# Soft-MoE after squared-ReLU attention: logits turned to slot rows in fp32, raw z for the first chunk, and the last half key tile in three products

## The chip, the cores and the metric

The kernel runs on one NeuronCore of a Trainium2 chip. The time is that of one execution on the device in microseconds; the median of three runs before the change is 1592.67 us. Engines are named as in the profile: PE (TensorE matrix products; PEld is its weight loads), DVE (VectorE), ACT (ScalarE), POOL (GpSimd) and SP (the queue that issues the DMAs). On PE one operand, the weights, is loaded into the 128 x 128 array and the other, the moving operand, streams through it. The array is used here mostly as two halves of 64 rows, which run separate products side by side, and in places as eight tiles of 64 x 32.

## The reference

```python
# B, S, D, d_qk = 8, 2496, 256, 64 ; E = 8 experts of 4 slots, F = 1024
scores = z @ z.T / S                    # per batch, (S, S)
attn = maximum(scores, 0) ** 2
x = u * (attn @ v)                      # (B*S, D) tokens, N = 19968
logits = x @ phi                        # (N, 32)
d = exp(logits - logits.max(0));  d /= d.sum(0) + 1e-9      # over tokens, per slot
slot_input = d.T @ x                    # (32, D)
slot_out[e] = maximum(slot_input[e] @ w1[e], 0) @ w2[e]     # 4 slots per expert
c = exp(logits - logits.max(1));  c /= c.sum(1) + 1e-9      # over slots, per token
out = c @ slot_out
```

All arrays are fp32. Everything up to `slot_input` is done in one pass over the tokens with running column maxima.

## The kernel before

**Split products.** Where speed matters, an fp32 operand is split into a rounded part of type fp32r (high) and the rest (low), and a product is three fp32r products: high x high, high x low, low x high. `load_z` (L70) and `load_v` (L83) load a raw tile and return a function that splits it: the high part is an ACT copy, the low part a DVE subtraction. z comes from the host as 64 rows twice (`zz`), so each half of the array has a copy; v comes in key tiles of 128, of which the 20th (`KT - 1`) holds the last 64 keys twice.

**Chunks and steps.** A batch's 2496 queries are worked in chunks of 512 and one of 448 (in the last batch 448 first, and the last 512 as two of 256). For a chunk there are five steps of four key tiles. `scores` (L184) computes two key tiles against the chunk, one in each half of the array, three products each, then ACT's Relu and Square and DVE's split into `ph` and `pl`. `attend` (L217) adds the products of v with `ph` and `pl` into the accumulator `acc`. It goes through a step's key tiles twice, in two turns `s`: a half of the array holds 64 of the 128 keys, and in the second turn the halves exchange the output columns, which lie in two banks of PSUM, PE's output memory. A turn's first product waits, through an empty POOL instruction, for the last product of the turn before (L233, L245 to L248). A key tile is three products for a half in each turn. For the 20th key tile the rows 64 to 127 of `ph` are overwritten with the low part (L213), and the half of rows 0 to 63 has two products in each turn and the other half one (L229, L230).

**Order.** `pe`, `act` and `dve` keep the order in which the program issues (`InOrder`, L38). Before each turn `between` (L478) runs the deferred DVE operations in `begin`, takes at most one item from `work`, and then issues a pair of scores of the *next* step with `pair` (L434). `middle` is run on ACT between the Relus and the Squares of the pair, `behind` after them. From the third turn of a chunk on one item of `work` is taken a turn, so up to eight a chunk.

**Opening.** `opening` and `next_split` (L95 to L104) load and split the first batch's z and v tiles between the first steps, with three raw tiles ahead. The second operand of the first chunk's scores is the split z tile 0, the weights are the split tile of the step.

**Tokens in groups.** `finish_chunk` (L274) multiplies the accumulator by u (with x's features on the partitions) and splits x into `xh` and `xl`. Tokens are taken in groups of 512, g = 0 to 38. A group has eight work items. Four are `group_tile` (L306): eight fp32r products with a matrix `rmat`, which holds an identity and phi, and turn a tile of 128 tokens and give its 32 logits at once; ACT copies both out (`lg`, `xt`), DVE adds up the logits (`lt`). One is empty. Three are steps of `group_soft` (L342): the maxima over a group's tokens by a transpose (`cmT`), spread back by another (`mbT`), exponentials `ex` and the combine weights `cw`, then the slot sums `sl`: eight fp32 products in 64 x 32 tiles of the array, added into `slot_acc` under the factor `al` for the change of the running maximum. All of this uses one PSUM buffer, `ms`.

**End.** `slot_acc` is summed over its four token tiles by products with the selection `esel` into `sT` (L514), the experts' two layers follow (`layer1`, `layer2`), `turn` (L402) transposes the combine weights, and `tokens` multiplies and stores 20 MB of output.

## Time and profile before

| | |
|---|---|
| median of three runs | 1592.67 us (1591.65 to 1595.54) |
| profiled execution | 1589.23 us, its span 1587.4 us |
| PE busy | 1534.9 us, 97% |
| DVE busy | 1258.0 us, 79% |
| ACT busy | 1103.6 us, 70% |
| slot products `sl` | 624 instructions, 26.0 us |
| products of the token tiles `tr` | 1248 instructions, 201.6 us |
| first attention product | starts at 15.92 us |
| end of the last product with u to the sums `sT` | 1499.04 to 1509.94 us |

A PE duration in the profile goes from the issue to the modelled end, so durations of products that run side by side or one behind the other overlap; what a product costs is read from the starts of its neighbours. An fp32 product is two instructions, an fp32r product and a transpose one. L46 is a helper's line through which all ordered instructions go, so operations are told apart by their tiles: `acc` attention, `sc` scores, `tr` token tiles, `sl` slot sums, `cT` the transposes of `turn`, `cmT` and `mbT` the maxima.

### The profile page before, as it was taken

How to read it: one execution, taken by the hardware profiler on the slowest of the kernel's cores; microseconds unless marked ns; L12 is line 12 of the kernel's file. 1: busy time of each engine (PE TensorE's matmuls, PEld its weight loads, DVE VectorE, ACT ScalarE, POOL GpSimd, SP SyncE). 2: the span in 40 equal slices, each digit the busy share in tenths (PEclk: the TensorE clock that was granted, in tenths of full speed). 3: DMA queues.
4: the chain of work that ended last, by engine and by line, in shares of the span. 5: the costliest groups of instructions: out<-in, count | busy, mean ns of one | idle time of the engine just before them, and what ended most of it. 6: DMA issues, size and time to landing. Idle time of an engine off the chain costs nothing.

```text
span 1587.4 us, 37236 instructions
## 1 busy us (share of the span) xinstructions
PE 1534.9 (97%) x14686; PEld 1300.1 (82%) x14686; DVE 1258.0 (79%) x2714; ACT 1103.6 (70%) x2346; POOL 3.3 (0%) x20
## 2 busy tenths in 40 slices
PE   6999999999999999999999999999999999999985
PEld 4787888889888888889888898888988889888853
DVE  6778877889779887888778887788878888777753
ACT  5677766778668776777667776677767777666543
POOL 0000000000000000000000000000000000000000
PEclk9999999999999999999999999999999999999985
DMA  3101110112001110111001120011100131000659
GB/s 120 48 21 46 55 34 15 35 46 68 21 15 46 48 48 14 28 46 55 28 15 41 47 67 15 20 47 48 42 14 28 46 119 43 26 8 8 232 217 388
DMA packets 36654, 91.55 MB, mean 58 GB/s; under 512 B 3712, under 2 KB 6272, under 8 KB 34432
## 3 DMA queue, kind: packets, MB, share of 16 engines
q1 hardware_dynamic: 36480, 89.18, 17.4%
q8 instruction: 116, 1.90, 0.5%
q14 instruction: 58, 0.48, 0.1%
HBM read 68.71 MB, written 20.45 MB: 56 GB/s over the span
## 4 chain that ended last, share of the span: by engine, by line
PE 86%; DVE 7%; DMA 2%; ACT 2%; issue 2%; DVEq 0%; SPq 0%; ACTq 0%
PE acc L46 62%; PE sc L46 16%; PE tr L46 5%; DMA outT<-ot 2%; DVE z L46 2%; DVE ph L46 1%; PE sl L46 1%; ACT r L46 1%; DVE pl L46 1%; PE h L542 1%; DVE x L46 0%; PE po L564 0%; DVE slot_acc L46 0%; DVE ot L624 0%; DVE v L46 0%
## 5 line engine op out<-in xcount | busy, mean ns | idle before, releaser
L46 PE MATMUL acc<-ph,v 64*128 64x512 f32 (+2 forms) x6464 | 1094.8, 382 | 0.7 <-DVE ph L46 0.7
L46 PEld LDWEIGHTS acc<-ph,v 64*128 64x128 f32 x6464 | 782.1, 184 | 90.3 <-DVE ph L46 1.8
L46 PE MATMUL acc<-pl,v 64*128 64x512 f32 (+2 forms) x3110 | 789.6, 381 | 0.0
L46 ACT ACTIVATE r<-sc 128x512 f32<-128x512 f32 (+2 forms) x820 | 428.4, 575 | 264.2 <-PE sc L46 253.1
L46 DVE TENSOR_TENSOR pl<-r,ph 128x512 fp32r<-128x512 f32 (+2 forms) x779 | 519.0, 666 | 51.8 <-PE acc L46 0.5
L46 DVE CAST ph<-r 128x512 fp32r<-128x512 f32 (+2 forms) x820 | 334.9, 408 | 205.4 <-ACT r L46 202.2
L46 PEld LDWEIGHTS acc<-pl,v 64*128 64x128 f32 x3110 | 448.0, 184 | 46.6 <-DVE pl L46 2.0
L46 ACT ACTIVATE r<-r 128x512 f32<-128x512 f32 (+2 forms) x820 | 455.2, 611 | 0.0
L46 PE MATMUL sc<-z,z 64*128 64x512 f32 (+2 forms) x1968 | 325.3, 389 | 12.4 <-ACT z L46 7.3
L46 PEld LDWEIGHTS sc<-z,z 64*128 64x128 f32 x1968 | 213.4, 185 | 44.8 <-issue 12.9
L46 ACT COPY lg<-tr 128x128 f32<-128x128 f32 x156 | 41.2, 264 | 124.6 <-PE tr L46 124.2
L46 PE MATMUL tr<-rmat,xl 64*128 64x256 f32 x624 | 100.0, 281 | 5.5 <-DVE xl L46 5.4
L46 PE MATMUL tr<-rmat,xh 64*128 64x256 f32 x624 | 101.6, 280 | 1.3 <-DVE slot_acc L46 1.3
L46 PEld LDWEIGHTS tr<-rmat,xh 64*128 64x128 f32 x624 | 84.9, 184 | 9.9 <-PE acc L46 3.3
L46 PE MATMUL sc<-z 64*128 64x512 f32 (+2 forms) x492 | 82.8, 395 | 5.3 <-ACT z L46 4.1
L46 PEld LDWEIGHTS tr<-rmat,xl 64*128 64x128 f32 x624 | 74.5, 184 | 10.8 <-DVE xl L46 8.5
L46 PEld LDWEIGHTS sc<-z 64*128 64x128 f32 x492 | 53.9, 188 | 13.6 <-ACT z L46 4.1
L46 DVE TENSOR_REDUCE lt<-lg 128x32 f32<-128x128 f32 x156 | 59.7, 383 | 0.8 <-ACT lg L46 0.5
L46 ACT COPY xt<-tr 128x256 f32<-128x256 f32 x156 | 59.0, 378 | 0.0
L46 DVE TENSOR_TENSOR v<-vr,v 128x512 fp32r<-128x512 f32 x80 | 54.8, 686 | 4.1 <-ACT v L46 3.8
L46 ACT CAST v<-vr 128x512 fp32r<-128x512 f32 x80 | 49.4, 617 | 12.0 <-PE sc L46 12.0
L46 DVE TENSOR_TENSOR z<-zr,z 64x512 fp32r<-64x512 f32 x80 | 55.0, 687 | 2.5
(81 smaller groups left out, 675.7 us busy)
## 6 DMA issues: line engine op xcount, KB each, us to landing
vr<-in_v SPq DMA_DIRECT2D x80, 256.0 KB, 2.6
w<-in_w SPq DMA_DIRECT2D x32, 512.0 KB, 5.6
outT<-ot SPq DMA_DIRECT2D x16, 1024.0 KB, 8.3
ut<-in_uT SPq DMA_DIRECT2D x31, 512.0 KB, 3.6
zr<-in_zz SPq DMA_DIRECT2D x40, 256.0 KB, 2.6
ut<-in_uT SPq DMA_DIRECT2D x8, 448.0 KB, 3.4
outT<-ot SPq DMA_DIRECT2D x4, 512.0 KB, 4.6
outT<-ot SPq DMA_DIRECT2D x2, 768.0 KB, 5.6
```

The lines of the kernel that those rows point to most:

```text
L46: return lambda *a, **k: self.tc.keep_in_program_order(f(*a, **k))
L542: nc.tensor.matmul(ps[j * NS : (j + 1) * NS], sT[:, c, (4 * eg + j) * NS : (4 * eg + j + 1) * NS], w_raw[w][:, k], start=(c == 0), stop=(c ...
```

## The change

- The last half key tile: the low part goes to a buffer of its own, and the three products of its 64 keys are dealt out so that both halves have two in the first turn and one in the second.
- The first chunk's scores are fp32 products of raw z tiles, all five of which stay in memory; their splits are issued later in the first and early in the second chunk, and only the v splits stand between the first steps.
- x is no longer split. Per group there are four work items in the place of eight. First the logits as 32 slots x 128 tokens, the four token tiles on four bands of 32 partitions (`lg`), with a maximum kept for each slot of each band; then the transposes of x (`tr`); then the transposes of logits and exponentials (`le`); then `sl` as before.
- The running maxima differ from band to band, so at the end a factor (`fac`) brings the four bands to one maximum, and `esel` times this factor (`fsel`) takes its place.
- x's columns come out in another order, and the host turns w1's rows accordingly.

```diff
-    zt, vt_ = {}, {}
+    zt, vt_, zraw = {}, {}, {}
     def load_z(b, j):
-        raw = raws.tile([P, 512], F32, tag="raw", name=f"zr_{b}_{j}")
+        raw = raws.tile([P, 512], F32, tag="zraw" if b == 0 else "raw", name=f"zr_{b}_{j}", bufs=NQ if b == 0 else NRAW)
         nc.sync.dma_start(raw, zz[b, :, j * 512 : (j + 1) * 512])
+        zraw[b, j] = raw
         def split():
             t = zt[b, j] = blk.tile([P, 2, 512], F32R, tag="blk", name=f"z_{b}_{j}")
             for h in (1, 0):
                 rows = HALF[h]
-                (dve.tensor_copy if h and b + j == 0 else act.copy)(t[rows, h], raw[rows])
+                act.copy(t[rows, h], raw[rows])
                 dve.tensor_sub(t[rows, 1 - h], raw[rows], f32(t[rows, h]))
         return split
...
-        raw = raws.tile([P, 2, D], F32, tag="raw", name=f"vr_{b}_{i}")
+        raw = raws.tile([P, 2, D], F32, tag="raw", name=f"vr_{b}_{i}", bufs=NRAW)
...
-    opening = [(load_z, 0)]
+    opening = []
     for p in range(NP):
-        opening += [(load_v, 2 * p), (load_v, 2 * p + 1)] + [(load_z, p + 1)] * (p + 1 < NP)
-    opened = []
-    def next_split():
-        while opening and len(opened) < NRAW - 1:
+        opening += [(load_z, p), (load_v, 2 * p), (load_v, 2 * p + 1)]
+    z_splits, v_splits = [], []
+    def open_loads(m):
+        while opening and (len(v_splits) < m or opening[0][0] is load_z):
             f, j = opening.pop(0)
-            opened.append(f(0, j))
-        opened.pop(0)()
+            (z_splits if f is load_z else v_splits).append(f(0, j))
...
-    rmat = xpool.tile([P, 2, 256], F32R, name="rmat")
-    NXT = 6
-    xt = [xpool.tile([P, 258], F32, name=f"xt{i}") for i in range(NXT)]
+    one = cpool.tile([1, 1], F32, name="one")
+    xt = [xpool.tile([P, 4, 258], F32, name=f"xt{i}") for i in range(2)]
...
         j, o, n, t0 = ch
         k0 = 4 * p + 2 * w
         ps = [sc_ps.tile([P, QC], F32, tag="sc", name=f"sc_{t0}_{k0 + h}") for h in range(2)]
-        zk, zq = zt[b, p], zt[b, j]
-        for m, (kl, ql) in enumerate(((0, 0), (0, 1), (1, 0))):
+        if t0 == 0:
             for h, rows in enumerate(HALF):
                 c = 2 * w + h
                 pe.matmul(
-                    ps[h][:, :n], zk[rows, h ^ kl, c * P : (c + 1) * P],
-                    zq[rows, h ^ ql, o : o + n], start=(m == 0), stop=(m == 2),
+                    ps[h], zraw[b, p][rows, c * P : (c + 1) * P], zraw[b, 0][rows],
+                    start=True, stop=True,
                 )
+        else:
+            zk, zq = zt[b, p], zt[b, j]
+            for m, (kl, ql) in enumerate(((0, 0), (0, 1), (1, 0))):
+                for h, rows in enumerate(HALF):
+                    c = 2 * w + h
+                    pe.matmul(
+                        ps[h][:, :n], zk[rows, h ^ kl, c * P : (c + 1) * P],
+                        zq[rows, h ^ ql, o : o + n], start=(m == 0), stop=(m == 2),
+                    )
         rs = []
         for h in range(2):
             r = wa.tile([P, QC], F32, tag="r", name=f"r_{t0}_{k0 + h}", bufs=5)
...
-            if kt < KT - 1:
+            if t0 == N - 256 and kt == KT - 1:
+                lo, rows = hi, HALF[1]
+            else:
                 lo = wa.tile([P, QC], F32R, tag="pl", name=f"pl_{t0}_{kt}", bufs=7)
-                dve.tensor_sub(lo[:, :n], r[:, :n], f32(hi[:, :n]))
-            else:
-                lo = None
-                dve.tensor_sub(hi[64:128, :n], r[64:128, :n], f32(hi[64:128, :n]))
+                rows = HALF[1] if kt == KT - 1 else slice(0, P)
+            dve.tensor_sub(lo[rows, :n], r[rows, :n], f32(hi[rows, :n]))
             pend[t0, kt] = hi, lo
         run(behind)
...
         j, o, n, t0 = ch
-        todo = [[], []]
+        todo = [[[], []], [[], []]]
         for kt in range(4 * p, 4 * p + 4):
             hi, lo = pend.pop((t0, kt))
             vt = vt_[b, kt // 2][:, kt % 2]
-            if lo is not None:
-                for h in range(2):
-                    todo[h] += [(vt[:, 0], hi), (vt[:, 1], hi), (vt[:, 0], lo)]
+            hh, lh, hl = (vt[:, 0], hi), (vt[:, 1], hi), (vt[:, 0], lo)
+            if kt < KT - 1:
+                for s in range(2):
+                    for h in range(2):
+                        todo[s][h] += [hh, lh, hl]
             else:
-                todo[0] += [(vt[:, 0], hi), (vt[:, 1], hi)]
-                todo[1] += [(vt[:, 0], hi)]
+                todo[0][0] += [hh, lh]
+                todo[0][1] += [lh, hl]
+                todo[1][0] += [hh]
+                todo[1][1] += [hl]
         for s in range(2):
             between(s)
             before = turns[-1:]
-            for i in range(len(todo[0])):
+            for i in range(len(todo[s][0])):
                 for h, rows in enumerate(HALF):
-                    if i >= len(todo[h]):
-                        continue
-                    vp, pp = todo[h][i]
+                    vp, pp = todo[s][h][i]
                     c = h ^ s
                     x = pe.matmul(
                         acc[:, c, :n], vp[rows, c * P : (c + 1) * P], pp[rows, :n],
                         start=(p == 0 and s == 0 and i == 0),
-                        stop=(p == NP - 1 and s == 1 and i == len(todo[h]) - 1),
+                        stop=(p == NP - 1 and s == 1 and i == len(todo[s][h]) - 1),
                     )
                     while before:
                         await_(x, before.pop())
...
-    xparts = {}
+    xg_ = {}
     def finish_chunk(b, ch, acc):
         _, _, n, t0 = ch
         ut = ut_.pop(t0)
-        x = wa.tile([P, 2, QC], F32, tag="x", name=f"x_{t0}", bufs=1)
-        dve.tensor_mul(x[:, :, :n], acc[:, :, :n], ut[:, :, :n])
         s = 0
         while s < n:
             g, o = divmod(t0 + s, 512)
             w = min(n - s, 512 - o)
-            if g not in xparts:
-                xparts[g] = tuple(
-                    wk.tile([P, 2, 512], F32R, tag=f"x{k}", name=f"x{k}_{g}") for k in "hl"
-                )
-            xh, xl = (t[:, :, o : o + w] for t in xparts[g])
-            xs = x[:, :, s : s + w]
-            def high(xh=xh, xl=xl, xs=xs):
-                act.copy(xh, xs)
-                begin.append(lambda: dve.tensor_sub(xl, xs, f32(xh)))
-            behind.append(high)
-            for t in range(o // P, (o + w) // P):
-                work.append(lambda g=g, t=t: group_tile(g, t))
+            if g not in xg_:
+                xg_[g] = wk.tile([P, 2, 512], F32, tag="xg", name=f"xg_{g}")
+            dve.tensor_mul(xg_[g][:, :, o : o + w], acc[:, :, s : s + w], ut[:, :, s : s + w])
             if o + w == 512:
-                it = group_soft(g)
-                work.extend([lambda: None] + [lambda it=it: next(it, None)] * 3)
+                it = group(g)
+                work.extend([lambda it=it: next(it, None)] * 4)
             s += w
...
+    def group(g):
+        x = xg_.pop(g)
+        ps = ms_ps.tile([P, 2, 512], F32, tag="ms", name=f"lg_{g}")
         for c in range(2):
...
+            for t in range(4):
                 for h, rows in enumerate(HALF):
                     pe.matmul(
...
+                        ps[t * NS : (t + 1) * NS, h, 0:P], phi_sb[rows, c],
+                        x[rows, c, t * P : (t + 1) * P], start=(c == 0), stop=(c == 1),
                     )
...
+        L = wk.tile([P, P], F32, tag="L", name=f"L_{g}")
+        E = wk.tile([P, P], F32, tag="E", name=f"E_{g}")
+        m = wk.tile([P, 4], F32, tag="m", name=f"m_{g}")
         mnew, mold = runmax[g % 2], runmax[(g + 1) % 2]
+        dve.tensor_copy(L, ps[:, 0, 0:P])
+        dve.tensor_add(L, L, ps[:, 1, 0:P])
         if g == 0:
...
+            dve.reduce_max(mnew, L, axis=AX.X)
         else:
...
+            dve.reduce_max(m[:, 0:1], L, axis=AX.X)
+            dve.tensor_max(mnew, m[:, 0:1], mold)
+            dve.tensor_sub(m[:, 2:3], mold, mnew)
+        dve.tensor_scalar_mul(m[:, 1:2], mnew, -1.0)
         def exps():
...
+            act.activation(E, L, AF.Exp, bias=m[:, 1:2])
             if g:
...
+                act.activation(m[:, 3:4], m[:, 2:3], AF.Exp)
         middle.append(exps)
         yield
...
+        ps = ms_ps.tile([P, 2, 512], F32, tag="ms", name=f"tr_{g}")
         for t in range(4):
+            for c in range(2):
+                for h, rows in enumerate(HALF):
+                    pe.transpose(
+                        ps[:, h, t * P + c * 64 : t * P + (c + 1) * 64],
+                        x[rows, c, t * P : (t + 1) * P], ident[rows, rows],
+                    )
+        xs = xt[g % 2]
+        act.copy(
+            xs[:, :, 0:D].rearrange("p t (h q) -> p h t q", h=2),
+            ps.rearrange("p h (t q) -> p h t q", q=P),
+        )
+        yield
+        ps = ms_ps.tile([P, 2, 512], F32, tag="ms", name=f"le_{g}")
+        for k, m_ in enumerate((L, E)):
+            for h, rows in enumerate(HALF):
+                pe.transpose(ps[:, h, k * 64 : (k + 1) * 64], m_[rows], ident[rows, rows])
+        le = wk.tile([P, 2, P], F32, tag="le", name=f"le_{g}")
+        act.copy(le, ps[:, :, 0:P])
+        rm = wk.tile([P, 2, 4], F32, tag="rm", name=f"rm_{g}")
+        lt = le[:, :, 0:64].rearrange("p h (b s) -> p h b s", s=NS)
+        cg = cw[:, g].rearrange("p (h b s) -> p h b s", b=2, s=NS)
+        def rows_of(i):
+            return rm[:, i].rearrange("p (h b) -> p h b", b=2)
+        def spread(i):
+            return rows_of(i).unsqueeze(3).to_broadcast([P, 2, 2, NS])
+        def combine():
+            dve.tensor_reduce(rows_of(0), lt, axis=AX.X, op=ALU.max)
+            dve.tensor_sub(cg, lt, spread(0))
+            middle.append(combine_exp)
+        def combine_exp():
+            act.activation(cw[:, g], cw[:, g], AF.Exp)
+            begin.append(combine_sum)
+        def combine_sum():
+            dve.tensor_reduce(rows_of(1), cg, axis=AX.X, op=ALU.add)
+            dve.tensor_scalar_add(rm[:, 1], rm[:, 1], 1e-9)
+            dve.reciprocal(rm[:, 1], rm[:, 1])
+            dve.tensor_mul(cg, cg, spread(1))
+        begin.append(combine)
+        yield
+        ps = ms_ps.tile([P, 2, 512], F32, tag="ms", name=f"sl_{g}")
+        for t in range(4):
+            e = le[:, t // 2, 64 + t % 2 * NS : 64 + (t % 2 + 1) * NS]
             for h, rows in enumerate(HALF):
                 pe.matmul(
...
+                    ps[t * NS : (t + 1) * NS, h, 0:258], e[rows], xs[rows, t], start=True, stop=True
                 )
         snew, sold = slot_acc[g % 2], slot_acc[(g + 1) % 2]
         if g == 0:
...
+            dve.tensor_copy(snew, ps[:, 0, 0:258])
         else:
             dve.scalar_tensor_tensor(
...
+                snew, sold, m[:, 3:4], ps[:, 0, 0:258], op0=ALU.mult, op1=ALU.add
             )
...
+        dve.tensor_add(snew, snew, ps[:, 1, 0:258])
...
-            next_split()
-            if w and opened:
-                next_split()
-    next_split()
+            v_splits.pop(0)()
+            open_loads(NRAW)
+        if b == 0 and z_splits and q % 2 and t0 + q >= 5:
+            z_splits.pop(0)()
+    open_loads(NRAW)
     for w in range(2):
         pair(0, w)
     constants()
...
     ep = ctx.enter_context(tc.tile_pool(name="ep", bufs=1))
     sfin = slot_acc[(NG - 1) % 2]
+    mfin = runmax[(NG - 1) % 2]
+    pm = ms_ps.tile([P, 512], F32, tag="ms", name="pm")
+    nc.tensor.transpose(pm[0:1, 0:P], mfin, ident)
+    mrow = ep.tile([1, 5, NS], F32, name="mrow")
+    nc.vector.tensor_reduce(
+        mrow[:, 4], pm[0:1, 0:P].rearrange("p (t s) -> p s t", s=NS), axis=AX.X, op=ALU.max
+    )
+    nc.vector.tensor_copy(mrow[:, 0:4], mrow[:, 4].unsqueeze(1).to_broadcast([1, 4, NS]))
+    nc.tensor.matmul(
+        pm[:, P : P + 1], mrow[:, 0:4].rearrange("p t s -> p (t s)"), one, start=True, stop=True
+    )
+    fac = ep.tile([P, 1], F32, name="fac")
+    nc.vector.tensor_sub(fac, mfin, pm[:, P : P + 1])
+    nc.scalar.activation(fac, fac, AF.Exp)
+    fsel = ep.tile([P, E_ * NS], F32, name="fsel")
+    nc.vector.tensor_scalar_mul(fsel, esel.rearrange("k e q -> k (e q)"), fac)
     sT = ep.tile([P, 2, E_ * NS], F32, name="sT")
     pt = ms_ps.tile([P, 512], F32, tag="ms", name="sT_ps")
     for c in range(2):
         nc.tensor.matmul(
-            pt[:, c * 256 : (c + 1) * 256], sfin[:, c * P : (c + 1) * P],
-            esel.rearrange("k e q -> k (e q)"), start=True, stop=True,
+            pt[:, c * 256 : (c + 1) * 256], sfin[:, c * P : (c + 1) * P], fsel,
+            start=True, stop=True,
         )
...
-            pn[:, eg : eg + 1], esel[:, 4 * eg : 4 * eg + 4].rearrange("k e q -> k (e q)"),
+            pn[:, eg : eg + 1], fsel[:, eg * P : (eg + 1) * P],
...
-    w1 = inputs["moe_w1"].reshape(2, 4, 2, P, 2, 512).transpose(0, 4, 2, 1, 3, 5).reshape(32, P, 512)
+    w1 = inputs["moe_w1"].reshape(2, 4, 2, 2, 64, 2, 512).transpose(0, 5, 3, 1, 2, 4, 6)
+    w1 = w1.reshape(32, P, 512)
```

More of the change, by code (lines that the diff above doesn't have):

```diff
@@ L136, in constants @@
         nc.sync.dma_start(phi_sb, phi.rearrange("(c p) s -> p c s", p=P))
-        dve.memset(f32(rmat), 0.0)
+        nc.gpsimd.memset(one, 1.0)
         for t in xt:
-            dve.memset(t[:, 256:258], 1.0)
-        for c in range(2):
-            o = 64 * (1 - c)
-            for rows in HALF:
-                dve.tensor_copy(rmat[rows, c, 64 - o : 128 - o], ident[rows, rows])
-            dve.tensor_copy(rmat[:, c, o : o + NS], phi_sb[:, c])
-            dve.tensor_sub(
-                rmat[:, c, o + NS : o + 2 * NS], phi_sb[:, c], f32(rmat[:, c, o : o + NS])
-            )
+            nc.gpsimd.memset(t[:, :, 256:258], 1.0)
     wk = moe.enter_context(tc.tile_pool(name="wk", bufs=2))
@@ L262, in attend_whole @@
             vt = vt_[b, kt // 2][:, kt % 2]
-            prods = [(vt[:, 0], hi), (vt[:, 1], hi)] + ([] if lo is None else [(vt[:, 0], lo)])
+            prods = [(vt[:, 0], hi), (vt[:, 1], hi)] + ([] if lo is hi else [(vt[:, 0], lo)])
             for c in range(2):
@@ L310, in group_tile @@
         for c in range(2):
-            for k, xp in enumerate((xh, xl)):
+            for t in range(4):
                 for h, rows in enumerate(HALF):
                     pe.matmul(
-                        ps[:, h, c * 64 : c * 64 + 256], xp[rows, c, t * P : (t + 1) * P],
-                        rmat[rows, c], start=(c + k == 0), stop=(c + k == 2), skip_group_check=True,
-                    )
-        i = (g * 4 + t) % NXT
-        if t == 0:
-            lt_[g] = (
-                wk.tile([P, 4, NS], F32, tag="lt", name=f"lt_{g}"),
-                wk.tile([P, 4, NS], F32, tag="cm", name=f"cm_{g}"),
-            )
@@ L323, in group_tile @@
-        lt, cm = lt_[g]
-        lg = wk.tile([P, 2, 64], F32, tag="lg", name=f"lg_{g}_{t}")
-        px = ps[:, :, 0:256].rearrange("p h (c q) -> p h c q", q=P)[:, :, :, 0:64]
-        act.copy(lg, ps[:, :, 64:128])
-        act.copy(xt[i][:, 0:D].rearrange("p (c h q) -> p h c q", c=2, h=2), px)
-        def logits():
-            dve.tensor_reduce(
-                lt[:, t], lg.rearrange("p h (k s) -> p s h k", s=NS), axis=AX.XY, op=ALU.add
-            )
-            if t == 3:
-                dve.tensor_reduce(
-                    cm[:, 0], lt.rearrange("p t s -> p s t"), axis=AX.X, op=ALU.max
-                )
-                dve.tensor_copy(cm[:, 1:4], cm[:, 0].unsqueeze(1).to_broadcast([P, 3, NS]))
@@ L340, in group_tile @@
-        begin.append(logits)
-    def group_soft(g):
-        del xparts[g]
-        lt, cm = lt_.pop(g)
-        pt = ms_ps.tile([P, 2, 512], F32, tag="ms", name=f"cmT_{g}")
-        for h, rows in enumerate(HALF):
-            pe.transpose(pt[:, h, 0:64], cm[rows].rearrange("p h s -> p (h s)"), ident[rows, rows])
+                        ps[t * NS : (t + 1) * NS, h, 0:P], phi_sb[rows, c],
+                        x[rows, c, t * P : (t + 1) * P], start=(c == 0), stop=(c == 1),
+                    )
@@ L354, in group_soft @@
-            dve.tensor_reduce(gm, pt[:, :, 0:64], axis=AX.XY, op=ALU.max)
-            dve.tensor_max(mnew, gm, mold)
-        mb = wk.tile([64, P], F32, tag="mb", name=f"mb_{g}")
-        dve.tensor_copy(mb, mnew[0:64].to_broadcast([64, P]))
-        yield
-        pb = ms_ps.tile([P, 2, 512], F32, tag="ms", name=f"mbT_{g}")
-        pe.transpose(pb[:, 0, 0:64], mb, ident[0:64, 0:64])
-        ex = wk.tile([P, 4, NS], F32, tag="ex", name=f"ex_{g}")
-        al = wk.tile([P, 1], F32, tag="al", name=f"al_{g}")
@@ L364, in group_soft @@
-        rm = wk.tile([P, 2, 4], F32, tag="rm", name=f"rm_{g}")
-        cg = cw[:, g].rearrange("p (t s) -> p t s", s=NS)
-        dve.tensor_sub(ex, lt, pb[:, 0, 0:NS].unsqueeze(1).to_broadcast([P, 4, NS]))
-        if g:
-            dve.tensor_sub(al, mold, mnew)
-        dve.tensor_reduce(rm[:, 0], lt, axis=AX.X, op=ALU.max)
-        dve.tensor_sub(cg, lt, rm[:, 0].unsqueeze(2).to_broadcast([P, 4, NS]))
+            dve.reduce_max(m[:, 0:1], L, axis=AX.X)
+            dve.tensor_max(mnew, m[:, 0:1], mold)
@@ L383, in group_soft @@
+        begin.append(combine)
[3 more added lines that the diff above has]
+            e = le[:, t // 2, 64 + t % 2 * NS : 64 + (t % 2 + 1) * NS]
             for h, rows in enumerate(HALF):
                 pe.matmul(
-                    psl[t * NS : (t + 1) * NS, h, 0:258], ex[rows, t],
-                    xt[(g * 4 + t) % NXT][rows], start=True, stop=True,
+                    ps[t * NS : (t + 1) * NS, h, 0:258], e[rows], xs[rows, t], start=True, stop=True
```

20 lines of the change are left out of this document (1 added, 19 removed).

## The prediction

> **What bounds the kernel now.** I read the page's busy shares and the chain that ended last first, then the span cut into stretches at the instants when a chunk of scores is finished.
>
> ```profile
> span 1587.4 us, 37236 instructions
> PE 1534.9 (97%) x14686; PEld 1300.1 (82%) x14686; DVE 1258.0 (79%) x2714; ACT 1103.6 (70%) x2346; POOL 3.3 (0%) x20
> ...
> PE 86%; DVE 7%; DMA 2%; ACT 2%; issue 2%; DVEq 0%; SPq 0%; ACTq 0%
> ```
>
> ```profile
> by line: PE acc L46 61.5%; PE sc L46 16.4%; PE tr L46 4.9%; DMA outT<-ot 2.1%; issue 1.9%; DVE z L46 1.5%; DVE ph L46 1.4%; PE sl L46 1.2%; ACT r L46 0.9%; DVE pl L46 0.9%; PE h L542 0.5%; DVE x L46 0.5%; PE po L564 0.5%; DVE slot_acc L46 0
> ```
>
> TensorE (PE) is the bound: 86% of the chain is its own work. The unit of account is a slot, in which the two 64-row halves of the array run one product each side by side. The chain of waits, in order of time, gives its length; the next fence holds rows of the stretches (columns: start:end, length, then busy time of PE, weight loads, DVE and ACT).
>
> ```profile
> 146.24 2.80 PE acc L46 x24
> ```
>
> ```profile
> 15.92:61.73 45.81, 38.12 (x305) 29.16 (x303) 31.82 (x63) 29.51 (x56) 0.00 (x0) 1.00 0.24 70
> 247.33:284.74 37.41, 37.41 (x349) 31.16 (x347) 28.26 (x63) 24.92 (x55) 0.00 (x0) 1.00 0.05 15
> 284.74:322.74 38.00, 37.70 (x349) 31.47 (x347) 33.60 (x72) 29.89 (x63) 0.00 (x0) 1.00 0.15 43
> 1017.45:1056.70 39.25, 38.92 (x359) 32.96 (x357) 33.61 (x72) 31.08 (x65) 0.00 (x0) 1.00 0.14 41
> ```
>
> 24 products in 2.80 us are 12 slots of 0.233 us. A chunk of 512 queries needs 10 x 3 slots of scores, 8 x 12 + 22 slots of attention, so 148 x 0.233 = 34.5 us, and about 2.7 us of work on one 512-token group (below): 37.2 us. The plain chunk takes 37.41, so there PE alone sets the pace. Chunks in which the next batch's z is split take 38.0 to 39.25, with DVE at 33.6; the first takes 45.8. So PE work counts in full everywhere, and DVE or ACT work only at the opening and in such chunks.
>
> **Part 1, the last half key tile.** Where does the odd product stand now?
>
> ```profile
> 245.25 0.60 PE L46 MATMUL acc<-ph,v 64*128 64x512 f32 x2
> 245.49 0.39 PE L46 MATMUL sc<-z 64*128 64x512 f32 x1
> 245.69 0.39 PE L46 MATMUL acc<-ph,v 64*128 64x512 f32 x1
> 245.72 0.83 PE L46 MATMUL sc<-z 64*128 64x512 f32 x4
> ```
>
> At 245.69 one half still does its 11th product of the turn while the other has gone on to scores at 245.49. The ahead half gains nothing: the half of rows 0 to 63, with 11 + 11 products over the last step's two turns, is the one that is always busy. After the change each half has 11 and 10, 21 slots for 22, with as many products. That is 0.233 us in 31 chunks of 512 queries, some 0.2 in the 8 of 448 and half of one in the 256: about -9 us. If the drift of the halves had already filled the gap it would be 0; bounds -9.2 and 0. I take -9, because nothing but a drift that lasts beyond a turn could fill it, and each turn waits for the one before. The subtraction on DVE keeps its 64 rows and only writes to another buffer: nothing.
>
> **Part 2, logits and transposes on PE, per group.** Removed: four token tiles of eight products each, two small turns (cmT, mbT). Added: 16 logit products in eight 64x32 tiles of the array, 16 transposes of x in halves, 4 transposes of logits and exponentials. `sl` stays.
>
> ```profile
> 78.98 0.28 PE L46 MATMUL tr<-rmat,xh 64*128 64x256 f32 x1
> ...
> 79.45 0.39 PE L46 MATMUL sc<-z,z 64*128 64x512 f32 x1
> ```
>
> ```profile
> 305.17 0.47 PE L46 MATMUL acc<-pl,v 64*128 64x512 f32 x2
> 305.57 0.67 PE L46 MATMUL sl<-xt,ex 64*32 64x258 f32 x16
> 306.17 0.97 PE L46 MATMUL sc<-z,z 64*128 64x512 f32 x6
> ```
>
> ```profile
> 924.50 0.28 PE L46 MATMUL cmT<-ident,cm 64*128 64x64 f32 x2
> 924.56 0.88 PE L46 MATMUL sc<-z,z 64*128 64x448 f32 x6
> ```
>
> ```profile
> 1498.14 0.60 PE L406 MATMUL cT<-ident,cw 128*128 128x128 f32 x4
> 1499.80 0.27 PE L406 MATMUL cT<-ident,cw 128*128 128x128 f32 x1
> 1505.71 0.14 PEld L46 LDWEIGHTS cmT<-ident,cm 64*128 64x128 f32 x2 [0.35 <-DVE cm L46]
> ```
>
> A token tile costs 79.45 - 78.98 = 0.47, four 1.88. A pair of 64-column transposes, its weights loaded under the slot before, costs 0.06. The group's `sl` costs 306.17 - 305.57 = 0.60 and 305.57 - 305.17 - 0.23 = 0.17 ahead of it: 0.77. Before: 1.88 + 0.06 + 0.06 + 0.77 = 2.77.
>
> After: the logits have the form of `sl`, eight tiles at once, 16 products of 128 columns for 8 of 258, so the same streaming: 0.77. The transposes in a row no longer hide their weights: four full ones take 0.60 and one 0.27, so 0.11 each, which I take per pair, since both halves' weights go in together in 0.14 (the weight-load row). Eight pairs: 7 x 0.11 + 0.06 = 0.83; logits and exponentials, two pairs: 0.17. Sum 0.77 + 0.83 + 0.17 + 0.77 = 2.54, that is -0.23 a group, x39 = -9 us. Bounds: all pairs at 0.06 give 0.48 + 0.12 in place of 1.00, -16 us more; 0.11 for each half in turn gives 2.20, +47 us. Each work item still has its own half step (2.8 us of attention) in which DVE or ACT empties the single PSUM buffer: no wait of PE from that unless DVE is late (a rival).
>
> The Trainium skill (TensorEngine Tiling (Array Packing), Key Properties) says that changing the tiling mode drains the array, which speaks against logits by slots: two such runs a group for one. By that rule the logits cost what `sl` does, 0.77, and without a drain 0.60, which would make the sum 7 us better; the trace agrees with the rule by the 0.17 us ahead of `sl`.
>
> **Part 3, what DVE and ACT are relieved of.**
>
> ```profile
> L46 ACT COPY lg<-tr 128x128 f32<-128x128 f32 x156 | 41.2, 264 | 124.6 <-PE tr L46 124.2
> L46 ACT COPY xt<-tr 128x256 f32<-128x256 f32 x156 | 59.0, 378 | 0.0
> L46 ACT CAST xh<-x 128x1024 fp32r<-128x1024 f32 x7 | 7.4, 1051 | 3.2 <-DVE x L46 3.2
> L46 DVE TENSOR_REDUCE lt<-lg 128x32 f32<-128x128 f32 x156 | 59.7, 383 | 0.8 <-ACT lg L46 0.5
> L46 DVE TENSOR_TENSOR xl<-x,xh 128x1024 fp32r<-128x1024 f32 x7 | 8.5, 1217 | 0.0
> L46 DVE TENSOR_REDUCE gm<-cmT 128x1 f32<-128x128 f32 x38 | 10.7, 282 | 0.0
> L624 ACT COPY ot<-pf 128x1024 f32<-128x1024 f32 x16 | 16.2, 1014 | 17.2 <-DMA outT<-ot 14.9 <-PE pf L618 2.0 <-ACT cp L608 0.3
> ```
>
> ACT loses 4 x (0.264 + 0.378) + 1.05 = 3.6 us a group and gains one copy of 1024 (1.01) and one of 256 (0.38): -2.2. DVE loses 4 x 0.383 + 1.22 = 2.75; its remaining small operations change kind (column maxima and their spreading go, copy, sum and row maxima come), about as many, each like gm's 0.28 or shorter. In the chunks with splits, which lag 37.2 by 0.8 to 2.0 us, DVE stands at 33.6 and comes late. Three of five chunks of seven batches have splits: 21 x 1.2 is some 25 us of lag in all. I take a third, -8 us; bounds -20 and 0. The longer copy (1.01 for 0.64) delays the following Relu by 0.4 us once a group; its result is needed some 5 us later, behind a turn's 2.8 us and another pair of scores, so it costs nothing there, 0.4 x 39 = 16 us if that cover were gone.
>
> **Part 4, the opening.** Rows of the timeline:
>
> ```profile
> 3.46 0.62 ACT L46 CAST z<-zr 64x512 fp32r<-64x512 f32 x1 [1.45 <-DMA zr<-in_zz]
> 5.40 1.22 PE L46 MATMUL sc<-z 64*128 64x512 f32 x4 [0.47 <-DVE z L46]
> 15.92 1.05 PE L46 MATMUL acc<-ph,v 64*128 64x512 f32 x4
> 24.93 0.73 PE L46 MATMUL sc<-z,z 64*128 64x512 f32 x4 [1.20 <-ACT z L46]
> 26.98 0.50 PE L46 MATMUL sc<-z,z 64*128 64x512 f32 x2 [1.32 <-DVE z L46]
> ```
>
> PE waits here for the two halves of a z split, the copy on ACT at 24.93 and the subtraction on DVE at 26.98, and likewise for the z tiles before and after. Raw z is there at 3.46. A pair of fp32 scores has two instructions a half; by `sl`, two instructions of 258 columns on each tile in at most 0.60, it takes at most 1.19, and surely no less than the 0.70 of three slots; the middle, 0.95, makes ten pairs 2.5 us longer. The first attention can start when Relu and squares of two pairs are through: pair one ends near 5.5 (from 3.46, two instructions of two slots' length at the slow early pace: the two slots at 5.40 take 1.22 with some 0.4 of latency, 0.4 or a little more each), pair two near 8.4, the third near 11.2, so 11.3 for 15.92. From there the rest of the 148 slots and the 2.5 us give some 37 us, and the slow pace until it ends some 1.7 more: 50 instead of 61.73. DVE and ACT are close behind (31.8 and 29.5 busy in that stretch, and the z work of three tiles still falls in it), so I take -11, bounds -14 and -3.
>
> **Part 5, the end.**
>
> ```profile
> 1498.35 0.69 DVE L46 TENSOR_TENSOR x<-acc,ut 128x512 f32<-128x512 f32 x1 [1.68 <-PE acc L46]
> 1508.85 0.48 DVE L46 SCALAR_TENSOR_TENSOR slot_acc<-slot_acc,al,sl 128x258 f32<-128x258 f32 x1 [0.65 <-PE sl L46]
> 1509.37 0.42 DVE L46 TENSOR_TENSOR slot_acc<-slot_acc,sl 128x258 f32<-128x258 f32 x1
> 1509.94 1.46 PE L514 MATMUL sT_ps<-esel,slot_acc 128*128 128x256 f32 x4 [1.26 <-DVE slot_acc L46]
> ```
>
> From the last product with u to sT 11.6 us now. After: the product with u 0.69 + logits 0.77 + two evacuations 0.56 + transposes 0.83 + copy 1.01 + 0.17 + copy 0.38 + sl 0.67 + 0.90 = 6.0, and 0.15 from engine to engine (1509.94 behind 1509.37 + 0.42) at seven hand-overs: 7.0. The new common maximum (a transpose, a reduction, a copy, a small product, a difference, an exponential, a product) is seven steps, each taken at gm's 0.28 with a hand-over: 3.0, so 10.0. I take -1, bounds -4 and +3. The w loads that run then are used later, from layer 1 on, and the output behind it is only shifted.
>
> **Sum.** -9 - 9 - 8 - 11 - 1 = -38 us. The profiled execution took 1589.23 us (span 1587.4 and 1.8 around it), 3.4 below the median of 1592.67: 1551 of its own kind, 1555 beside the median.
>
> **Rivals.** A: weights of the two row halves load one behind the other in fp32 transposes: +47 us, 1602. For it: no row shows long runs of such pairs. Against: the cmT row, two loads in 0.14. It decides against the change from +38 us, 0.97 us a group. B: DVE is late for the new chain (copy, sum, maxima before PE may reuse the buffer), and PE waits in each group as it once did 2.0 us (the row below): 39 x 2.0 = +78, 1633. Against: all such waits together are 7.4 us from 61.73 to 1456.69, and DVE has less to do.
>
> ```profile
> PEld tr L46 <- DVE xl L46: 7.4, 9, 2.0
> ```
>
> C: the opening is bound by DVE and ACT, which keep all their splits: -3 for -11, 1563. D: the freed slot was filled already, so that part doesn't do what it says: 1564. E: transposes at 0.06 a pair throughout: 1539.
>
> **How the numbers follow.** Forecast 0.64, its own range 1543 to 1568; C 0.07; D 0.07; E 0.08; A 0.08; B 0.06. The range 1535 to 1588 leaves out A and B and no more than a few in a hundred below. A measurement of this kernel tells some 0.3% (5 us) from no change: faster 0.86, and A may land within 5 us of the old time in half its cases, 0.04; slower 0.10.
>
> **What would show it.** Plain chunks of 512 at 36.9 us or a little less; the last step's turns with as many products in both halves; 16 transposes within 1.1 us, logits as short as `sl`; no z wait before the first chunk's scores and its end near 50; sT 10 us behind the last product with u. Wrong: transposes of 1.7 us or more a group, DVE waits ahead of `le` or `tr`, a first chunk that still ends past 58.

## The result, and the profile after

The changed kernel takes 1529.76 us (1529.70 to 1530.05, four runs), the kernel before 1592.16 us (1589.32 to 1595.54, four runs beside it): a ratio of 0.9608, interval 0.9589 to 0.9627. The gain is 62 us where 38 were forecast, and the time lies 5 us below the forecast range of 1535 to 1588. The profiled execution of after is one of 1529.76 us, with a span of 1528.0.

The page of after, its busy shares and the shares of the chain that ended last:

```profile
PE 1499.4 (98%) x15332; PEld 1203.0 (79%) x15332; DVE 1158.0 (76%) x2466; ACT 1033.0 (68%) x2043; POOL 3.2 (0%) x23
...
PE 96%; DMA 2%; DVE 1%; ACT 0%; issue 0%; DVEq 0%; SPq 0%; ACTq 0%
```

PE's part of the chain has gone from 86% to 96%: nearly all that stood between its products is gone. Next come stretches of the span, cut where the last product with u of a chunk starts; columns as in the prediction's stretches. Before, from the end of chunk 0 on (38 chunks, the last two chunks of 256, the way to `sT`, the rest):

```profile
61.73:1456.69 1394.96, 1387.56 (x13057) 1190.90 (x13055) 1141.70 (x2469) 1003.53 (x2135) 0.00 (x0) 1.00 0.13 37
1456.69:1498.35 41.66, 39.70 (x619) 37.62 (x618) 32.62 (x99) 27.63 (x89) 0.00 (x0) 1.00 0.40 135
1498.35:1509.94 11.59, 8.36 (x73) 5.42 (x72) 7.97 (x21) 5.47 (x14) 0.00 (x0) 1.00 1.02 405
1509.94:1587.40 77.46, 55.23 (x625) 34.08 (x625) 34.74 (x46) 29.20 (x41) 0.00 (x0) 0.68 0.73 300
```

After, with chunk 0 from its first attention on, a plain chunk and one with splits ahead of them:

```profile
11.10:50.66 39.56, 39.56 (x303) 34.58 (x301) 33.14 (x60) 31.79 (x60) 0.00 (x0) 1.00 0.26 76
226.10:262.70 36.60, 36.60 (x366) 28.65 (x364) 25.89 (x57) 23.10 (x46) 0.00 (x0) 1.00 0.06 16
262.70:299.80 37.10, 37.10 (x370) 29.06 (x368) 31.16 (x65) 28.44 (x55) 0.00 (x0) 1.00 0.15 44
50.66:1403.50 1352.84, 1352.84 (x13671) 1089.28 (x13667) 1050.60 (x2247) 935.66 (x1843) 0.00 (x0) 1.00 0.14 38
1403.50:1441.60 38.10, 38.10 (x628) 36.58 (x628) 29.05 (x90) 24.51 (x77) 0.00 (x0) 1.00 0.45 150
1441.60:1452.90 11.30, 8.78 (x111) 5.96 (x107) 7.71 (x24) 5.04 (x11) 0.00 (x0) 1.00 1.02 382
1452.90:1528.00 75.10, 53.42 (x624) 33.24 (x624) 33.76 (x42) 29.41 (x42) 0.00 (x0) 0.70 0.75 313
```

| stretch | before | after | difference | forecast |
|---|---|---|---|---|
| to the end of chunk 0 | 61.73 | 50.66 | -11.1 | -11 (part 4) |
| 38 chunks | 1394.96 | 1352.84 | -42.1 | -26 (parts 1 to 3) |
| last two chunks | 41.66 | 38.10 | -3.6 | not told apart |
| to `sT` | 11.59 | 11.30 | -0.3 | -1 (part 5) |
| from `sT` on | 77.46 | 75.10 | -2.4 | 0 |

From 11.1 to 1441.6 us PE is busy without a break in all three rows that cover it; before, 9.4 us of the first two rows shown were idle. The missing gain is 16 us in the 38 chunks and 5 behind them. The timeline of one group on PE in after (start, duration, operation, count) shows where most of the 16 comes from:

```profile
767.94 0.40 PE L46 MATMUL acc<-pl,v 64*128 64x512 f32 x2
768.27 0.67 PE L46 MATMUL lg<-xg,phi_sb 64*32 64x128 f32 x32
768.87 0.96 PE L46 MATMUL sc<-z,z 64*128 64x512 f32 x6
769.67 0.63 PE L46 MATMUL acc<-ph,v 64*128 64x512 f32 x4
...
772.24 0.39 PE L46 MATMUL acc<-pl,v 64*128 64x512 f32 x2
772.47 0.66 PE L46 MATMUL tr<-ident,xg 64*128 64x64 f32 x16
772.93 0.94 PE L46 MATMUL sc<-z,z 64*128 64x512 f32 x6
773.71 0.63 PE L46 MATMUL acc<-ph,v 64*128 64x512 f32 x4
...
776.52 0.22 PE L46 MATMUL le<-ident,L 64*128 64x64 f32 x2
776.58 0.23 PE L46 MATMUL le<-ident,E 64*128 64x64 f32 x2
776.62 0.94 PE L46 MATMUL sc<-z,z 64*128 64x512 f32 x6
777.39 0.63 PE L46 MATMUL acc<-ph,v 64*128 64x512 f32 x4
...
779.96 0.40 PE L46 MATMUL acc<-pl,v 64*128 64x512 f32 x2
780.29 0.67 PE L46 MATMUL sl<-xt,le 64*32 64x258 f32 x16
780.89 0.96 PE L46 MATMUL sc<-z,z 64*128 64x512 f32 x6
781.69 0.63 PE L46 MATMUL acc<-ph,v 64*128 64x512 f32 x4
```

The eight pairs of transposes take 772.93 - 772.47 = 0.46 us, 0.058 a pair; `le` takes 776.62 - 776.52 = 0.10. The logits take 768.87 - 768.27 = 0.60 and 768.27 - 767.94 - 0.233 = 0.10 ahead of them, `sl` the same: 0.70 each. Together 1.96, where 2.54 was forecast. Some of it comes back behind these runs: the three slots of scores that follow take 0.80, 0.78, 0.77 and 0.80 to the next attention product in place of 0.70, in all 0.35. That makes 2.31 a group, and the pace of the plain chunk agrees: 36.60 less 147 slots of 0.2333 is 2.30. The kernel before gives 37.41 - 148 x 0.2333 = 2.88 by the same reckoning. So PE's work on a group fell by 0.58, where the forecast had -0.23.

The last half key tile in after:

```profile
757.68 0.62 PE L46 MATMUL acc<-ph,v 64*128 64x512 f32 x3
757.91 0.39 PE L46 MATMUL acc<-pl,v 64*128 64x512 f32 x1
758.14 0.86 PE L46 MATMUL sc<-z,z 64*128 64x512 f32 x6
758.84 0.63 PE L46 MATMUL acc<-ph,v 64*128 64x512 f32 x4
```

No attention product stands among the scores any more: the two halves enter the scores together at 758.14 and leave them 0.70 later. The opening, and the way to `sT`:

```profile
3.53 2.08 PE L46 MATMUL sc<-zr 64*128 64x512 f32 x4 [3.53 <-DMA zr<-in_zz]
...
10.13 1.41 PE L46 MATMUL acc<-ph,v 64*128 64x512 f32 x1
...
1441.58 0.69 DVE L46 TENSOR_TENSOR xg<-acc,ut 128x512 f32<-128x512 f32 x1 [1.75 <-PE acc L46]
1449.87 0.27 PE L506 MATMUL pm<-ident,runmax 128*1 128x128 f32 x1
1452.87 1.13 PE L524 MATMUL sT_ps<-fsel,slot_acc 128*128 128x256 f32 x4 [0.91 <-DVE fsel L519]
```

The first pair starts as soon as raw z is there, and the first attention product is issued at 10.13 instead of 15.92. At the end the common maximum takes from 1449.87 to 1452.87, 3.0 us.

### The profile page after: what moved, and what is told of

The parts are those of the page before. It is cut to its first block, busy times and chain, and to the rows that moved or that the text cites. A ratio compares the mean times of both kernels' runs of the same rounds, so it can differ in the third digit from the quotient of the medians.

```text
span 1528.0 us, 38187 instructions
## 1 busy us (share of the span) xinstructions
PE 1499.4 (98%) x15332; PEld 1203.0 (79%) x15332; DVE 1158.0 (76%) x2466; ACT 1033.0 (68%) x2043; POOL 3.2 (0%) x23
## 3 DMA queue, kind: packets, MB, share of 16 engines
q8 instruction: 121, 1.98, 0.5%
## 4 chain that ended last, share of the span: by engine, by line
PE 96%; DMA 2%; DVE 1%; ACT 0%; issue 0%; DVEq 0%; SPq 0%; ACTq 0%
PE acc L46 70%; PE sc L46 19%; DMA outT<-ot 2%; PE lg L46 2%; PE sl L46 2%; PE tr L46 1%; PE h L552 0%; PE po L574 0%; DVE ot L634 0%; PE le L46 0%; PE pf L628 0%; DMA zr<-in_zz 0%; PE cT L396 0%; DVE cw L397 0%; PE so L605 0%
## 5 line engine op out<-in xcount | busy, mean ns | idle before, releaser
L46 PE MATMUL acc<-ph,v 64*128 64x512 f32 (+2 forms) x6384 | 996.7, 383 | 0.0
L46 PEld LDWEIGHTS acc<-ph,v 64*128 64x128 f32 x6384 | 617.5, 185 | 120.2 <-issue 0.2
L46 PE MATMUL acc<-pl,v 64*128 64x512 f32 (+2 forms) x3190 | 639.4, 382 | 0.0
L46 DVE TENSOR_TENSOR pl<-r,ph 128x512 fp32r<-128x512 f32 (+4 forms) x819 | 546.0, 667 | 66.8 <-PE acc L46 1.4
L46 PEld LDWEIGHTS acc<-pl,v 64*128 64x128 f32 x3190 | 318.8, 185 | 57.5
L46 PE MATMUL sc<-z,z 64*128 64x512 f32 (+2 forms) x1920 | 275.8, 391 | 0.0
L46 PEld LDWEIGHTS sc<-z,z 64*128 64x128 f32 x1920 | 170.9, 185 | 46.0 <-issue 18.2
L46 DVE TENSOR_TENSOR xg<-acc,ut 128x512 f32<-128x512 f32 (+7 forms) x71 | 49.7, 736 | 1.8 <-PE acc L46 1.8
L46 ACT CAST z<-zr 64x512 fp32r<-64x512 f32 x80 | 49.6, 620 | 1.9
L46 ACT COPY xt<-tr 128x1024 f32<-128x1024 f32 x39 | 39.5, 1013 | 11.7 <-PE tr L46 11.7
L628 PE MATMUL pf<-cp,soh 32*128 32x512 f32 (+2 forms) x176 | 27.2, 587 | 10.7 <-ACT ot L634 8.4
L628 PEld LDWEIGHTS pf<-cp,soh 32*128 32x128 f32 x176 | 14.1, 258 | 22.9 <-ACT ot L634 16.5
```

Source lines behind the costliest of these rows:

```text
L46: return lambda *a, **k: self.tc.keep_in_program_order(f(*a, **k))
L628: nc.tensor.matmul(pf[t // 2][:, t % 2, :ng], a[rows, c], parts[g0][rows, k, :ng], start=(m == 0), stop=(m == 2), tile_position=(t * NS, 0),)
```

## The experiments

Every run stands against the changed kernel's 1529.76 us unless something else is said; ratios are to the kernel before, which ran beside each of them (1588.7 to 1595.7 us). The eleven kernels either undo a part, put work back, or go one step further.

**The old dealing of the last half key tile.**

```diff
-                todo[0][0] += [hh, lh]
-                todo[0][1] += [lh, hl]
-                todo[1][0] += [hh]
-                todo[1][1] += [hl]
+                for s in range(2):
+                    todo[s][0] += [hh, lh]
+                    todo[s][1] += [hl]
...
+                    if i >= len(todo[s][h]):
+                        continue
```

> Only the dealing of the last half key tile is put back: 11 products in each turn for the half of rows 0 to 63, 10 for the other. If the busier half sets the pace (the forecast's first part), 40 chunks lose a slot again: +8.9 us on the changed kernel's 1529.8, so 1538.7. If the drift of the halves fills the gap: 1530.

1538.18 us (1537.93 to 1538.33), ratio 0.9652 [0.9637, 0.9666]: 8.4 us lost, 7.0 of them in the 38 chunks: about 0.22 in a chunk of 512 queries and 0.06 in one of 448. Another 1.7 came behind `sT`, where the two kernels do the same work (more on this below). The slot was not filled by a drift of the halves: rival D falls.

**The first chunk's scores from split z.** The splits are issued just ahead of their pairs, as before the change.

```diff
-                act.copy(t[rows, h], raw[rows])
+                (dve.tensor_copy if h and b + j == 0 else act.copy)(t[rows, h], raw[rows])
...
-        if t0 == 0:
+        if False:
...
-        if b == 0 and z_splits and q % 2 and t0 + q >= 5:
+        if i < NP and w and z_splits:
             z_splits.pop(0)()
...
     open_loads(NRAW)
+    z_splits.pop(0)()
```

> Only the opening's arithmetic is put back: the first chunk's scores are made from split z again, each z tile split just ahead of its step. The forecast's term is 11 us: 1541. If DVE and ACT bound the opening either way, 3 us: 1533.

1545.1 us (1543.54 to 1546.78), ratio 0.9692 [0.9673, 0.9711]: 15.3 us lost, and chunk 0 ends at 64.8 instead of 50.7. Two stretches of this kernel, the row of a wait in the second, and the same stretch of the opening in the kernel before:

```profile
43.00:46.50 3.50, 1.81 (x14) 0.85 (x10) 3.26 (x6) 2.18 (x4) 0.00 (x0) 1.00 0.28 75
46.50:53.30 6.80, 5.90 (x28) 4.62 (x30) 3.57 (x7) 2.63 (x5) 0.00 (x0) 0.50 0.13 42
```

```profile
47.40 0.79 PE L46 MATMUL sc<-z,z 64*128 64x512 f32 x2 [1.39 <-DVE z L46]
```

```profile
42.80:46.20 3.40, 1.81 (x14) 0.84 (x10) 3.16 (x6) 2.18 (x4) 0.00 (x0) 1.00 0.27 77
46.20:53.00 6.80, 5.80 (x50) 4.73 (x52) 3.81 (x8) 4.42 (x9) 0.00 (x0) 1.00 0.28 81
```

PE waits for z again, and after a stretch of 3.50 us in which it is busy for 1.81 the granted clock stands at one half for 6.8 us. In the kernel before the same wait left PE just as idle, and the clock stayed full, so this fall is not explained by the wait alone. At half clock 6.8 us do the work of 3.4, so up to 3.4 of the 14.1 us are the clock's, and the other 10.7 are the waits and the slower splits: what part 4 was forecast to be worth. Rival C (a gain of 3) falls.

**Both undone,** so that the group's part is left alone; the two edits above together.

> Both the key tile and the opening put back, so that what is left of the change is the work on logits and transposes. If the parts add up, 1529.8 + 8.9 + 11 = 1550, that is 42 us under the kernel before, where the forecast had 18 for this part with the relief of DVE and ACT and the end. If the parts hide one another, less than that is lost: 1540 or below.

1551.88 us (1549.44 to 1552.63), ratio 0.9735 [0.9719, 0.9751]: 22.1 us lost, where the two alone make 8.4 + 15.3 = 23.7. Within the scatter of the runs the parts add up, and the work on groups, with what it relieves DVE and ACT of and with the end, is worth 40 us against before. That is where the forecast (-9, -8 and -1) was too small.

**Transposes of x over the full array.** Eight transposes of 128 columns take the place of sixteen in halves; x's columns and w1's rows then stand as before the change.

```diff
-                for h, rows in enumerate(HALF):
-                    pe.transpose(
-                        ps[:, h, t * P + c * 64 : t * P + (c + 1) * 64],
-                        x[rows, c, t * P : (t + 1) * P], ident[rows, rows],
-                    )
+                pe.transpose(ps[:, c, t * P : (t + 1) * P], x[:, c, t * P : (t + 1) * P], ident)
```

> The 16 transposes of x in halves (64 moving columns each) are replaced by 8 of the whole array (128 moving columns each); w1's rows go back to their old order, everything else stays. If the moving columns set a transpose's pitch, eight at the 0.108 us of the combine weights' transposes take 0.87 instead of 0.47 us a group: +15.6 us, 1545. If the load of 128 weight columns sets it (the forecast's pricing), eight loads in a row cost what eight pairs of loads did: 1530.

1556.55 us (1553.67 to 1556.83), ratio 0.9763 [0.9747, 0.9779]: 26.8 us lost, more than either expectation. Its timeline:

```profile
785.31 0.40 PE L46 MATMUL acc<-pl,v 64*128 64x512 f32 x2
785.64 1.09 PE L46 MATMUL tr<-ident,xg 128*128 128x128 f32 x8
786.66 0.97 PE L46 MATMUL sc<-z,z 64*128 64x512 f32 x6
```

From 785.64 to 786.66 the eight take 1.02, and 785.64 - 785.31 - 0.233 = 0.10 stands ahead of them: 1.12 for 0.46. 0.66 x 39 = 25.7 is nearly all of the loss. Taken one by one they start 0.109 us apart, which is the price that the forecast took from `cT`; the other 0.25 (1.12 less eight times 0.109) goes with the change between halves and the full array.

**Transposes of x issued twice,** into the same place, so that the second set only costs time: `for _ in range(2):` round the loop.

> Each of the 16 transposes of x is issued twice, to the same place. The price of eight pairs in a row on the path of PE is then read directly: at the 0.058 us a pair seen in the changed kernel +0.47 a group, +18 us, 1548; at the forecast's 0.11 a pair +0.83 a group, +32 us, 1562.

1547.14 us (1546.96 to 1549.08), ratio 0.9717 [0.9696, 0.9739]: 17.4 us for 39 sets of eight pairs, 0.45 a set and 0.056 a pair. The timeline agrees:

```profile
780.65 1.16 PE L46 MATMUL tr<-ident,xg 64*128 64x64 f32 x32
781.62 0.70 PE L46 MATMUL sc<-z,z 64*128 64x512 f32 x4
```

16 pairs in 0.97 are 0.061 a pair. The forecast's 0.11 would have cost 0.83 x 39 = 32 us and is refuted.

**DVE's time put back:** with each of a group's four work items one subtraction of 128 x 512 (0.69 us, 2.75 a group) whose output nothing uses.

```diff
+        begin.append(lambda: dve.tensor_sub(idle_out, idle_in, idle_in))
```

> With each of the four work items of a group DVE gets one more subtraction of 128x512 (0.69 us, output not used), so that 2.75 us a group, which the change took from DVE, are back; PE's work is unchanged. If DVE's relief is worth what the forecast took, +8 us: 1538; if the whole lag of the chunks with splits hung on it, +20 us: 1550; if PE's own work is all that counted, 1530.

1535.52 us (1534.39 to 1536.70), ratio 0.9642 [0.9620, 0.9664]: 5.8 us lost, 3.3 in the 38 chunks: 0.8 more in each chunk of the kind of 262.70 above (37.9 for 37.1), of which 0.4 is made up for in the next (35.7 for 36.1).

**ACT's time put back:** with each item one copy of 128 x 448 (2.2 a group), unused too.

```diff
+        behind.append(lambda: act.copy(idle_out[:, 0:448], idle_in[:, 0:448]))
```

> The same for ACT: one more copy of 128x448 (0.54 us) after the squares with each work item, 2.2 us a group. If ACT's share of the relief counts, up to +8 us: 1538; if only DVE was late, 1530.

1533.61 us (1530.89 to 1534.41), ratio 0.9627 [0.9605, 0.9649]: 3.8 us lost, none in the 38 chunks (1352.8 again); 2.1 on the way to `sT`, which goes through ACT, and 1.8 behind it.

**Both put back.**

> DVE's 2.75 us and ACT's 2.2 us a group are both put back (outputs not used), so both engines carry about what they did before while PE's work is the changed kernel's. If the 12 us of lag that went from the chunks with splits hung on the two engines' load, they return here: 38 chunks from 1352.8 to 1365 and the run near 1543. If they hung on the order of the old chain (the low part of x and the maxima had to be ready before PE could go on), the two runs alone add up: +3.3 in the 38 chunks and 1537 to 1539 in all.

1542.25 us (1541.43 to 1542.69), ratio 0.9681 [0.9667, 0.9696]: 12.5 us lost. The time is near the first expectation, but only 7.0 us of it came in the 38 chunks, where that expectation had 12. Its 38 chunks:

```profile
49.90:1409.70 1359.80, 1359.18 (x13668) 1101.66 (x13665) 1132.81 (x2395) 998.05 (x1991) 0.00 (x0) 1.00 0.13 38
```

7.0 us more than after, where DVE alone gave 3.3 and ACT alone nothing; DVE and ACT are about as busy here as in the kernel before (1132.81 and 998.05 against 1141.70 and 1003.53), but PE is idle for only 0.6 us instead of 7.4. The 7 us show in the waits of PE's weight loads in that stretch (total, times, longest):

```profile
PEld acc L46 <- DVE pl L46: 7.2, 22, 0.6
```

After has no such wait; the other waits of the weight loads are the same in sum in both (49 us). So with the old load DVE is late with `pl`, and that load costs the changed kernel 7 us. The kernel before, under about the same load, shows much less of this wait:

```profile
PEld acc L46 <- DVE pl L46: 1.7, 4, 0.4
```

There the delay sat in the old chain of the groups (see part 3 below), which does not come back in this run, since x is not split again; that order by itself was not tried.

**Slot sums of a group beside the logits of the next,** in one PSUM buffer and one run of 64 x 32 tiles: a version that goes further than the change. The sums get their exponentials and x from the group before; the last group's stay by themselves, and one of the four work items of the others is empty.

```diff
         ps = ms_ps.tile([P, 2, 512], F32, tag="ms", name=f"lg_{g}")
+        add = late.pop()(ps, P) if late else None
...
         dve.tensor_add(L, L, ps[:, 1, 0:P])
+        if add:
+            add()
...
-                work.extend([lambda it=it: next(it, None)] * 4)
+                step = lambda it=it: next(it, None)
+                work.extend([step, lambda: None, step, step] + [step] * (g == NG - 1))
```

> A group's slot sums are issued in one run with the next group's logits, in the same PSUM buffer beside them, so that the array changes to its eight small tiles and back once a group and not twice. If each change costs what the rows show (0.09 ahead of the run, about 0.1 behind it and 0.1 more in the scores that follow), -0.2 to -0.3 a group, 8 to 11 us less: 1520. If the changes cost nothing, 1530; if DVE's longer turn (both evacuations) makes PE wait, above 1530.

1519.78 us (1519.37 to 1522.40), ratio 0.9548 [0.9523, 0.9574]: 10.0 us better than the changed kernel, and 11.7 in the 38 chunks, 0.31 a group. Its timeline:

```profile
798.01 0.40 PE L46 MATMUL acc<-pl,v 64*128 64x512 f32 x2
798.34 0.67 PE L46 MATMUL lg<-xt,le 64*32 64x258 f32 x16
798.80 0.70 PE L46 MATMUL lg<-xg,phi_sb 64*32 64x128 f32 x32
799.42 0.96 PE L46 MATMUL sc<-z 64*128 64x512 f32 x6
```

0.10 ahead and 1.08 for both runs, 1.18 in place of 0.70 + 0.70; one run fewer also leaves out the 0.10 in the scores behind it. The products are the same in number, so what is saved is what stands around a run in another tile shape. The Trainium skill (TensorEngine Tiling (Array Packing), Key Properties) says that a change of the tiling mode drains the array. This run agrees that such changes cost time, 0.31 us for the two (there and back) that it saves; that the cost is a drain it does not show.

**Products of zeros before the first scores:** seven pairs into an unused accumulator, so that the clock is up earlier.

```diff
+    for _ in range(7):
+        for h, rows in enumerate(HALF):
+            pe.matmul(wps[:, h], idle[rows, 0:P], idle[rows], start=True, stop=True)
```

> Seven pairs of products of a zeroed tile are issued ahead of the first scores, while PE waits for z, so that it is busy from about 1.2 us on. In the changed kernel full pace is granted from 14.9 us. If the early work brings it forward to about 8, some 3 us of the stretch from 9 to 15 are saved: 1527. If the clock follows something else, or DVE and ACT bound the opening, 1530.

1529.85 us (1529.44 to 1530.63), ratio 0.9605 [0.9590, 0.9619]: nothing. Two stretches of its opening:

```profile
6.00:9.50 3.50, 1.98 (x6) 0.59 (x4) 1.43 (x3) 3.10 (x7) 0.00 (x0) 1.00 0.99 339
9.50:12.90 3.40, 3.32 (x11) 2.94 (x13) 3.30 (x7) 3.27 (x8) 0.00 (x0) 0.50 0.96 350
```

In the kernel after, the three slots of a key tile take 1.28 us until 14.8 us and 0.70 from there on, so it starts at half pace, although the clock column of its row 11.10:50.66 reads 1.00. Here the clock is full from 6.0 us, but the scores start at 4.60 instead of 3.53, and PE then waits for Relu and squares (0.68 and 0.92 us), is busy for 1.98 of 3.50 us, and has half the clock for the next 3.40. Chunk 0 ends 0.6 us earlier, which the time of the whole kernel does not show.

**The last two together.**

> The slot sums beside the next group's logits (1519.8 alone) and the early products together. If they add up, 1517; if the early products bring nothing, 1520.

1520.09 us (1518.95 to 1520.69), ratio 0.9542 [0.9526, 0.9557]: as the slot sums beside the logits alone.

## Why the prediction was right and wrong

The direction was right, and the forecast's size was not: -38 for -59.4 us between the two profiled spans.

**Part 1 (-9)** had the mechanism right and the size nearly: undoing it costs 8.4 us, but only 7.0 of them lie in the 38 chunks, mostly because a chunk of 448 gave 0.06 where 0.2 was priced.

**Part 2 (-9)** is where the prediction failed. Its failing step reads "so 0.11 each, which I take per pair". The price came from `cT`, whose transposes move 128 columns through the full array; those of the change move 64 through each half and go at 0.058 a pair (0.061 in the longer row of the run that issues them twice), 0.46 for eight and 0.10 for `le`, in place of 0.83 and 0.17. That is 0.44 x 39 = 17 us. Issuing them twice shows the price by itself, and the full transposes show that the price of `cT` was not wrong for what it was read from. Rows and columns were changed together in that experiment, so which of them halves the price stays open. The nearer row was quoted in the prediction and used only as a bound: `cmT`, the same 64 x 64 form, at 0.06. Rival E, with just that price, was right on the transposes (its 1539 lacks the other misses below) and was given 0.08. The logits cost what `sl` does, as forecast, but both at 0.70 instead of 0.77, 5 us more. Not foreseen at all were the 0.35 us a group in the scores behind such runs; before it was 2.88 - 2.77 = 0.11, so 0.24 x 39 = 9 us came back. Net, PE's group work gained 0.58 x 39 = 23 us instead of 9.

**Part 3 (-8)** was within its bounds and 5 us short. Of the 42.1 us of the 38 chunks 7.0 belong to part 1 and 0.58 x 38 = 22 to part 2, which leaves 13. Of these 7.4 are time in which PE stood idle in the kernel before, all of it in the old chain of the groups (total, times, longest), and which after does not have:

```profile
PE tr L46 <- DVE xl L46: 4.8, 4, 1.7
PE cmT L46 <- DVE cm L46: 1.3, 4, 0.3
PE tr L46 <- DVE slot_acc L46: 1.3, 4, 0.4
```

Putting the engines' time back costs 7.0 us, but by the wait for `pl` and with PE idle for 0.6. So the runs show that DVE's and ACT's load matters to the changed kernel; how much of the 13 us came from the lighter load and how much from the shorter chain is not shown, and some 6 of them stay open.

**Part 4 (-11)** was right: 11.1 in the trace, first attention product and end of chunk 0 within about a microsecond of 11.3 and 50, and 10.7 by undoing it, without the clock's part. That the end of chunk 0 came out so close is in part luck: the first attention product was issued 1.2 us earlier than priced, and from there to the end of the chunk it took 40.5 us where 38.7 was priced.

**Part 5 (-1)** was too small as a sum over the end: 6 us came. The way to `sT` that it worked out, at 10.0, took 11.3; the common maximum took its 3.0, so the rest of the chain was priced 1.3 too low. But 3.6 us came in the last two chunks, which part 5 left out and part 3 did not reach: before, PE was idle there for 1.96 us, after for none. The 2.4 us behind `sT` were not forecast. The changed kernel and the experiments all do the same work there, and their profiles show either 75.0 to 75.2 us (after among them) or 76.4 to 77.0. So up to 1.9 of the 2.4 can be such a difference; what makes it is open.

**Rivals.** A (weights of the halves one behind the other, from 0.97 us a group) falls: the whole run of transposes takes 0.46. B (DVE late) falls: PE has no idle time in the 38 chunks, even though the one buffer `ms` is still emptied by DVE and ACT. C and D fell in the experiments.

So the total was off by 21 us: 14 in part 2, 5 in part 3 and 5 at the end, less 2 in the slots, which gave 7.0 of the 9 in the 38 chunks (with rounding). The range took in the transposes' lower price (1539) by itself, but not together with a larger relief and a gain at the end, although the prediction's own bounds for these (-20 and -4) reached that far.

## What to carry to other kernels

Price an instruction from the row with the same tile shape and the same moving columns, even when that row is a short one; a longer row of another form may be twice off. Where PE alone sets the pace, add to a run in another tile shape what stands ahead of it and in the products behind it (0.1 us each here), and put such runs together: that alone was worth another 10 us. Warming the clock early was worth nothing here: it fell again behind the waits that followed.
